# A linear-attention block times a SwiGLU block: when half of the query divisions run, the order in which a segment's right operands are split, and a priority on the first operands

## The chip, the cores and the metric

The kernel runs on one core of a Trainium2 chip. The metric is the device time of one execution in microseconds (us); lower is better. The kernel before took 2384.69 us, the median of three runs (2384.14 to 2392.65).

## The reference, cut to what matters

Shapes: x is 2048 x 1024, wqkv 1024 x 3072, wo 1024 x 1024, w1 and w3 1024 x 3584, w2 3584 x 1024, all float32; 32 heads of 32 columns.

```python
xn = layernorm(x)
q, k, v = split(xn @ wqkv)                       # per head
phi = lambda t: where(t > 0, t + 1, exp(t)) + 1e-6
kv = phi(k).T @ v;  z = sum over tokens of phi(k)
s = (phi(q) @ kv / (phi(q) @ z + 1e-6)) @ wo     # linear attention
g = silu((silu(xn @ w1) * (xn @ w3)) @ w2)       # SwiGLU
out = x + s * g
```

Both blocks, the attention that ends in s and the SwiGLU that ends in g, read the normalised x.

## The kernel before, in words

Every matrix product is float32 made of three reduced-precision matmuls (`mm3`, lines 97 to 99): each operand is split into a high part (copied by ScalarE, ACT) and a low remainder (subtracted by VectorE, DVE). On top of that, products of 2 x 2 blocks are made with seven products in place of eight: a right operand comes as B11, T2, B21, T1, T3, B22, T4, a left one as A11, S2, A12, S1, S3, S4, A22, the letters T and S being sums and differences of blocks.

**First layer** (up to line 849). Two halves of 1024 tokens, h = 0 and 1; in each, gemms for k and v, then q (4 pairs of column blocks), then gate and up, g and u (14 pairs). A gemm (`gemm`, line 399) is seven products of 12 matmuls each, in the order a, b, c, d, a, c, d: the letter is the PSUM bank, and a, c and d are accumulated into twice, so the second product on c or d waits until DVE has read the first (lines 436 and 442). Behind each product `catch_up` (line 387) advances a queue of side jobs by one step; a step is a `yield`. The jobs of half 1 are `attention_work` (line 823): denominators for the queries of half 0, the merging of kv with wo, 16 divisions for the queries of half 0 (called H0 below), denominators of half 1, and 16 divisions of half 1 (H1). `divide` (line 753) loads a tile by four DMAs on SP's queue (lines 762 and 764), waits two steps, does one DVE instruction on the loaded data (line 770) and four sums (lines 607 to 611), and stores the tile to `qs_d` from POOL's queue (line 773). Its tile has three buffers, and `go_on` loads two jobs ahead, so that a load waits until the store of the job three earlier has landed. Hidden activations go to `ho_d`; the sums of them (line 637) are stored from POOL in half 0 and from SP in half 1.

**Second layer** (from line 852): four segments B0 to B3 over the hidden columns (B0 has 2 blocks of 128 per product, the others 4), and an attention segment s. Each segment has 8 token groups m of 256 tokens, each with seven products in `ORDER` (numbered e = 0 to 6 below): 6 matmuls in B0, 12 later. The right operand of a product (`Segment.right`, line 873) lies in a buffer by its name with one copy, loaded and split in pieces of two blocks (128 x 1024), two pieces in B1 to s. The left one (`Segment.left`, line 880) comes by one DMA on SP's queue into one of five buffers, four products ahead, and is split by ACT (line 895) and DVE (line 896). While the last group (m = 7) of a segment runs, the next segment's right operands are placed, loaded and split, each right behind the product that frees its buffer (lines 1029 to 1031). DVE also reads the PSUM banks (lines 939 to 955).

The order on each engine is made when the kernel is built: a scheduler with its own simulated timeline orders the instructions by priority (program order, unless changed) and readiness. `tc.issue_after(mark)` forbids it to put the enclosed instructions ahead of the mark. At run time every engine and every DMA queue works in the order that was fixed then.

Of the kernel before, what the change touches and what calls it, by code (L numbers as in the profile page):

```python
# [9 lines left out]
F32 = mybir.dt.float32  # L10
# [6 lines left out]
P = 128  # L17
# [5 lines left out]
def tile_linear_attention_times_swiglu(  # L23
# [375 lines left out]
    def gemm(B, A, use, early=False, paired=False, own=False):  # L399
# [67 lines left out]
        next(stages, None)  # L467
        if name[0] in "gu":
            catch_up(copied, added)
# [144 lines left out]
    def hidden(h, pair):  # L614
# [18 lines left out]
        def sums(c):  # L633
            o = [small(f"hs{h}_{pair}_{c}_{e}") for e in range(2)]
            for e, _ in enumerate(four_sums(sg[0, c], sg[1, c], *o)):
                queue = nc.gpsimd if h == 0 or pair == NF // 2 - 1 else nc.sync
                queue.dma_start(out=ho_d[i][2 * h + c][:, :, 3 + 2 * e:5 + 2 * e, k],  # L637
                                in_=o[e].rearrange("p (g n s) -> p g n s", n=2, s=P))
# [113 lines left out]

    def divide(m, k):

        c, cols = m // NT, slice(m % NT * 2 * P, (m % NT + 1) * 2 * P)

        def load():
            t = job_tile([P, 4, 2 * P], f"qd{m}_{k}")
            for e in range(2):
                j = k + e * (ND // 2)  # L760
                rows = r_d[c][j * (P // DH):(j + 1) * (P // DH), cols]
                nc.sync.dma_start(out=t[:, 2 + e], in_=bass.AP(
                    tensor=rows.tensor, offset=rows.offset, ap=[[C, P // DH], [0, DH], [1, 2 * P]]))
                nc.sync.dma_start(out=t[:, e], in_=pq_d[j // JG][c][:, j % JG, cols])
            return t

        def steps(t):
            for _ in range(2):
                yield True
# [53 lines left out]
    def attention_work():  # L823
# [5 lines left out]
        work += [j for c in H1 for j in denominators(c)]  # L829
        work += [divide(m, k) for m in range(NT * H1[0], NT * NCH) for k in range(ND // 2)]  # L830
        yield from go_on(work)
# [26 lines left out]
    def late_pool(name, bufs=1):  # L858
        return ctx.enter_context(tc.tile_pool(name=name, bufs=bufs, reuse_waits="tile"))

    pacc, pu, pw, pacc2, pt, px = (late_pool(*how) for how in (
        ("pacc",), ("pu",), ("pw",), ("pacc2",), ("pt", 4), ("px", 5)))

    class Segment:
# [8 lines left out]
        def right(self, n):  # L873

            y = self.Y[n]
            for k in range(0, self.nk, 2):
                nc.sync.dma_start(out=y[:, 1, k:k + 2].bitcast(F32), in_=self.right_of(n, slice(k, k + 2)))
                split(y[:, e, k:k + 2].rearrange("p k c -> p (k c)") for e in range(2))

        def left(self, m, n):  # L880
            t = px.tile([P, 2, ND // 2, P], FR, tag="x", name=f"X{PARTNER[n]}{self.name}_{m}")
            x_ = t[:, :, :self.nk]
            loads[:] = [nc.sync.dma_start(out=x_[:, 1].bitcast(F32), in_=self.left_of(m, PARTNER[n]))]
            split(x_[:, e] for e in range(2))
            return x_
# [6 lines left out]
    def split(pair):  # L892
        hi, lo = pair
        src = lo.bitcast(F32)
        nc.scalar.copy(out=hi, in_=src)  # L895
        return nc.vector.tensor_sub(out=lo, in0=src, in1=hi.bitcast(F32))  # L896

    loads = []

# [10 lines left out]

    def temp(name):
        return pt.tile([P, C], F32, tag="t", name=name)

# [46 lines left out]
    def attention_tokens(seg, m):  # L960
# [29 lines left out]
        yield bd, True  # L990
        c22 = temp(f"c22{name}")
        A.copy(out=c22, in_=bd)
# [3 lines left out]
        yield bd, False  # L996
        c12 = temp(f"c12{name}")
        V.tensor_add(out=c12, in0=bd, in1=u)
# [16 lines left out]
    for n in PRODUCTS:  # L1015
        layers[0].place(n)
    for j, n in enumerate(ORDER):
        if j < AHEAD:
            fetch(j)
        layers[0].right(n)  # L1020
    for i, seg in enumerate(segments):
        for m in range(NG):
            parts = attention_tokens(seg, m) if seg is attention else layer_tokens(seg, m, i == 0)
            for e, n in enumerate(ORDER):
                j = (i * NG + m) * len(ORDER) + e
                fetch(j + AHEAD)
                b, start = next(parts)
                seg.product(b, X.pop(j), n, start)
                if m == NG - 1 and i + 1 < len(segments):
                    segments[i + 1].place(n)  # L1030
                    segments[i + 1].right(n)
            next(parts)
            if i == 2 and m < ADDED:
                lay_x(m)


# [21 lines left out]
```

## Time and profile before

| | |
|---|---|
| three timed runs, median | 2384.69 us |
| the profiled execution's own time | 2392.09 us |
| its span, and what lies around it | 2390.3 us, 1.8 us |
| busy: TensorE (PE), DVE, ACT, POOL | 98%, 69%, 40%, 10% of the span |
| mean granted clock of TensorE | 0.994 |
| HBM traffic over the span | 172 GB/s |

The span is the time from the first to the last instruction of one profiled execution. The profiled execution was 7.4 us longer than the median; durations are read from it, and sums are made against its own time. Windows are given in microseconds from the start of the span. PE counts as busy while matmuls that overlap run, so the number of matmuls in a window says more than the busy share. L123 is a line of the kernel before; the same statement stands one or two lines earlier or later in the kernel after. SPq is SP's DMA queue: instructions there issue transfers.

### The profile page before, as it was taken

The page shows a single profiled execution, that of the slowest core. Times are in us where ns is not written, and L with a number is a line of the kernel's source. Part 1 is how long each engine was busy: PE and PEld are TensorE (multiplying, and loading weights), DVE is VectorE, ACT ScalarE, POOL GpSimd, SP SyncE. Part 2 cuts the span into 40 slices and gives each one's busy share as a digit, 9 for nine tenths or more (in the row PEclk, how much of TensorE's full clock was granted, in tenths as well). Part 3 has the DMA queues.
Part 4 walks back from the last instruction along what each step waited for, and adds up shares of the span by engine and source line. Part 5 has one row for each costly group of instructions (what it writes and reads, how often), then busy time and mean ns, then how long its engine had stood idle before and what let it go on. Part 6 is the DMA issues. An engine that isn't in the chain of part 4 may idle for free. (4 is left out here: it accounts for less than half of the span.)

```text
span 2390.3 us, 29773 instructions
## 1 busy us (share of the span) xinstructions
PE 2338.0 (98%) x10544; PEld 1931.3 (81%) x10544; DVE 1652.1 (69%) x2941; ACT 953.5 (40%) x1612; POOL 240.6 (10%) x305
## 2 busy tenths in 40 slices
PE   6999999999999999999999999999999999999999
PEld 5788888888888888888888878887768878788787
DVE  8755878888887566567877877886564564644744
ACT  5434554433233244345343323332562342544522
POOL 3000011211212100000111110111000000000000
PEclk9999999999999999999999999999999999999999
DMA  3211455577663582134444765575463464633666
GB/s 124 88 53 54 150 172 169 187 243 243 227 232 129 189 331 106 64 105 134 166 152 168 229 211 182 166 244 180 126 215 97 140 208 150 247 97 104 229 149 157
DMA packets 289590, 395.45 MB, mean 165 GB/s; under 512 B 17008, under 2 KB 210800, under 8 KB 289328
## 3 DMA queue, kind: packets, MB, share of 16 engines
q1 hardware_dynamic: 265920, 315.67, 40.8%
q0 software_dynamic: 23520, 77.87, 9.5%
q8 instruction: 82, 1.34, 0.2%
q14 instruction: 68, 0.56, 0.1%
HBM read 271.58 MB, written 140.25 MB: 172 GB/s over the span
## 5 line engine op out<-in xcount | busy, mean ns | idle before, releaser
L629 POOL DMA_DIRECT2D ho_d<-sg x56 | 51.0, 911 | 502.2 <-DVE sg L624 439.8
L921 POOL DMA_DIRECT2D out<-acc x14 | 12.0, 861 | 683.3 <-DVE acc L969 683.3
L586 POOL DMA_DIRECT2D pq_d<-pq x32 | 17.6, 550 | 483.8 <-DVE pq L475 480.7
L637 POOL DMA_DIRECT2D ho_d<-hs x60 | 54.5, 909 | 44.8 <-DVE hs L608 30.0
L896 DVE TENSOR_TENSOR XS1B<-XS1B 128x512 fp32r<-128x512 f32 (+1 forms) x32 | 20.0, 624 | 44.5 <-ACT XS1B L895 44.5
L98 PE MATMUL aB<-B11B,XA11B 128*128 128x512 f32 x112 | 44.6, 398 | 4.2 <-DVE B11B L896 4.2
L627 POOL DMA_DIRECT2D ho_d<-sg x56 | 37.6, 672 | 101.8 <-DVE sg L624 80.6
L99 PE MATMUL dB<-T1B,XS1B 128*128 128x512 f32 x112 | 43.9, 392 | 3.9 <-DVE XS1B L896 3.9
L896 DVE TENSOR_TENSOR XA12B<-XA12B 128x512 fp32r<-128x512 f32 (+1 forms) x32 | 20.0, 624 | 37.7 <-ACT XA12B L895 37.7
L97 PE MATMUL dB<-B22B,XS4B 128*128 128x512 f32 x112 | 44.1, 394 | 1.3 <-DVE acc L939 0.7
L97 PE MATMUL aB<-B11B,XA11B 128*128 128x512 f32 x112 | 44.6, 398 | 0.6 <-ACT XA11B L895 0.6
L99 PE MATMUL cB<-T4B,XA22B 128*128 128x512 f32 x112 | 43.9, 392 | 1.3 <-DVE XA22B L896 1.3
L770 DVE SCALAR_TENSOR_TENSOR qd<-qd 128x512 f32<-128x512 f32 x32 | 21.9, 683 | 33.5 <-DMA qd<-pq_d 33.4
L99 PE MATMUL aB<-B11B,XA11B 128*128 128x512 f32 x112 | 44.5, 397 | 0.5 <-DVE XA11B L896 0.5
L97 PE MATMUL cB<-T3B,XS3B 128*128 128x512 f32 x112 | 43.8, 391 | 0.7 <-ACT cB L945 0.7
L97 PE MATMUL cB<-T4B,XA22B 128*128 128x512 f32 x112 | 43.8, 391 | 0.6 <-ACT XA22B L895 0.6
L99 PE MATMUL cB<-T3B,XS3B 128*128 128x512 f32 x112 | 43.8, 391 | 0.4 <-DVE XS3B L896 0.4
L99 PE MATMUL aB<-B21B,XA12B 128*128 128x512 f32 x112 | 43.9, 392 | 0.2 <-DVE XA12B L896 0.2
L97 PE MATMUL aB<-B21B,XA12B 128*128 128x512 f32 x112 | 43.7, 390 | 0.5 <-ACT uB L942 0.5
L99 PE MATMUL bB<-T2B,XS2B 128*128 128x512 f32 x112 | 44.1, 393 | 0.0
L97 PE MATMUL bB<-T2B,XS2B 128*128 128x512 f32 x112 | 44.0, 393 | 0.0
L98 PE MATMUL bB<-T2B,XS2B 128*128 128x512 f32 x112 | 44.0, 393 | 0.0
(5750 smaller groups left out, 8102.5 us busy)
## 6 DMA issues: line engine op xcount, KB each, us to landing
qs_d<-qd POOLq DMA_DIRECT2D x32, 512.0 KB, 5.5
ho_d<-hs POOLq DMA_DIRECT2D x60, 256.0 KB, 5.3
ho_d<-sg POOLq DMA_DIRECT2D x56, 256.0 KB, 4.2
w<-in_B_w SPq DMA_DIRECT2D x56, 256.0 KB
wt_d<-w SPq DMA_DIRECT2D x28, 512.0 KB
ho_d<-hs SPq DMA_DIRECT2D x52, 256.0 KB
pq_d<-pq POOLq DMA_DIRECT2D x32, 256.0 KB, 2.9
a_dS<-xo SPq DMA_DIRECT2D x16, 512.0 KB
```

The lines of the kernel that those rows point to most:

```text
L97: nc.tensor.matmul(acc, lhsT=wh, rhs=ah, start=start, stop=False, skip_group_check=True)
L98: nc.tensor.matmul(acc, lhsT=wh, rhs=al, start=False, stop=False, skip_group_check=True)
L99: nc.tensor.matmul(acc, lhsT=wl, rhs=ah, start=False, stop=stop, skip_group_check=True)
L586: nc.gpsimd.dma_start(out=pq_d[j // JG][2 * h + c][:, j % JG], in_=pq)
L627: nc.gpsimd.dma_start(out=ho_d[i][2 * h + c][:, :, 0, k], in_=halves[:, :, 0])
L629: nc.gpsimd.dma_start(out=ho_d[i][2 * h + c][:, :, 1:3, k], in_=halves)
L637: queue.dma_start(out=ho_d[i][2 * h + c][:, :, 3 + 2 * e:5 + 2 * e, k], in_=o[e].rearrange("p (g n s) -> p g n s", n=2, s=P))
L770: nc.vector.scalar_tensor_tensor(t[:, :2], t[:, :2], 1e-6, t[:, 2:], op0=ALU.add, op1=ALU.mult)
L896: return nc.vector.tensor_sub(out=lo, in0=src, in1=hi.bitcast(F32))
L921: nc.gpsimd.dma_start(out=out[r0:r0 + P, :].rearrange("p (n c) -> p n c", c=C), in_=a, accum_op=ALU.add)
```

## The change

Five edits:

- The 16 divisions of H1 leave `attention_work`. They become a job of their own in the second layer, with tiles from the pool `pt` (two buffers in place of three) and six steps of waiting; `catch_up` advances it by one step behind each product of the groups m = 1 to 6 in the segments B0 to B3. A division is seven steps, so 16 take 112 steps: 42 in B0, 42 in B1, 28 in B2. Each step is issued behind the newest left operand's load and split.
- The divisions of H0 stay and wait four steps in place of two.
- The gemms of q advance the side jobs by one more step (half 0 and half 1).
- The stores of the hidden sums in half 1 all go from POOL's queue (52 were on SP's).
- The right operands' pieces are still loaded at the same places, but their splits are put into a list and taken from it one or two at a time, seven in five products, from m = 7, e = 2 of the segment before to m = 0, e = 4, each behind the split of the newest left operand. The first segment's operands are issued at a higher priority.

Cut to its core:

```diff
-        if name[0] in "gu":
+        if name[0] in "guq":
             catch_up(copied, added)
...
-                queue = nc.gpsimd if h == 0 or pair == NF // 2 - 1 else nc.sync
-                queue.dma_start(out=ho_d[i][2 * h + c][:, :, 3 + 2 * e:5 + 2 * e, k],
+                nc.gpsimd.dma_start(out=ho_d[i][2 * h + c][:, :, 3 + 2 * e:5 + 2 * e, k],
...
-    def divide(m, k):
+    def divide(m, k, tile_of=job_tile, wait=4):
...
-            for _ in range(2):
+            for _ in range(wait):
                 yield True
...
-        work += [divide(m, k) for m in range(NT * H1[0], NT * NCH) for k in range(ND // 2)]
...
-                split(y[:, e, k:k + 2].rearrange("p k c -> p (k c)") for e in range(2))
+                yield lambda k=k: split(y[:, e, k:k + 2].rearrange("p k c -> p (k c)") for e in range(2))
...
-            split(x_[:, e] for e in range(2))
+            marks[:] = split(x_[:, e] for e in range(2))
...
+    def late_work():
+        yield from go_on([divide(m, k, temp, 6) for m in range(NG // 2, NG) for k in range(ND // 2)])
+
+    jobs.append((late_work(), False))
...
+    with tc.high_priority(offset=150):
+        for j, n in enumerate(ORDER):
+            if j < AHEAD:
+                fetch(j)
+            for made in layers[0].right(n):
+                made()
+
+    pending, turn = [], 0
+
+    def make_right():
+        for _ in range(7 * (turn + 1) // 5 - 7 * turn // 5):
+            if pending:
+                with ExitStack() as behind:
+                    for mark in marks:
+                        behind.enter_context(tc.issue_after(mark.ins))
+                    pending.pop(0)()
+
...
                 fetch(j + AHEAD)
+                if m == NG - 1 and e >= 2 or m == 0:
+                    make_right()
+                    turn += 1
+                else:
+                    turn = 0
                 b, start = next(parts)
                 seg.product(b, X.pop(j), n, start)
                 if m == NG - 1 and i + 1 < len(segments):
                     segments[i + 1].place(n)
-                    segments[i + 1].right(n)
+                    pending.extend(segments[i + 1].right(n))
+                elif m and i < len(layers):
+                    catch_up(*marks, *loads)
```

What it moves is seen in three places.

DVE in half 1 of the first layer, where an H0 division's first instruction (on a tile qd) meets the reads of the banks of a gemm u (c22u is read from bank c on one line and from bank d on another). Before:

```order
L436 TENSOR_TENSOR c22u1_6__11364<-cu1_6__11326,uu1_6__11306 128x512
L770 SCALAR_TENSOR_TENSOR qd2_2_11369<-qd2_2_11369 128x512
L90 TENSOR_TENSOR T3g1_7__11343<-wg1_7__11135,T3g1_7__11343 128x512
L611 TENSOR_TENSOR qd2_0_11232<-qd2_0_11232 128x128
L607 TENSOR_TENSOR qd2_2_11369<-qd2_2_11369 128x128
L610 TENSOR_TENSOR qd2_2_11369<-qd2_2_11369 128x128
L442 TENSOR_TENSOR c22u1_6__11364<-du1_6__11327,c22u1_6__11364 128x512
```

And the one place after where such an instruction follows closest on the store that its tile waits for (that of qd0_2, ten rows above this piece's fifth):

```order
L436 TENSOR_TENSOR c22u1_5__11021<-cu1_5__10989,uu1_5__10964 128x512
L90 TENSOR_TENSOR T3g1_6__11006<-wg1_6__10809,T3g1_6__11006 128x512
L442 TENSOR_TENSOR c22u1_5__11021<-du1_5__10990,c22u1_5__11021 128x512
L769 SCALAR_TENSOR_TENSOR qd0_3_10877<-qd0_3_10877 128x512
L769 SCALAR_TENSOR_TENSOR qd1_1_11095<-qd1_1_11095 128x512
L90 TENSOR_TENSOR B21g1_6__11023<-wg1_6__10809,B21g1_6__11023 128x512
L624 TENSOR_TENSOR sg1_5_11_10895<-c22u1_5__11021,sg1_5_11_10895 128x512
```

The instruction on the loaded tile stood ahead of the read of bank d; now it stands behind it.

SP's queue in B0, group 3 (an X tile is a left operand; the number behind B0 is the group). Before:

```order
L883 DMA XA12B0_3_14059<-ho_d0_1_87 128x256
L883 DMA XS1B0_3_14070<-ho_d0_1_87 128x256
L883 DMA XS3B0_3_14082<-ho_d0_1_87 128x256
L883 DMA XS4B0_3_14097<-ho_d0_1_87 128x256
L883 DMA XA22B0_3_14108<-ho_d0_1_87 128x256
```

After:

```order
L881 DMA XA12B0_3_13904<-ho_d0_1_87 128x256
L881 DMA XS1B0_3_13915<-ho_d0_1_87 128x256
L761 DMA qd4_2_13854<-r_d2_123 128x1x256
L763 DMA qd4_2_13854<-pq_d0_2_80 128x256
L761 DMA qd4_2_13854<-r_d2_123 128x1x256
L763 DMA qd4_2_13854<-pq_d1_2_84 128x256
L881 DMA XS3B0_3_13933<-ho_d0_1_87 128x256
L881 DMA XS4B0_3_13953<-ho_d0_1_87 128x256
```

The four loads of a late division now stand between two left operands; their first one waits for the store of the division two earlier. There are six such places in B0 (the first holds two divisions, the last stands between the two pieces of B11 of B1), and nine in B1 and B2.

DVE at the change from B0 to B1 (names as in the second layer, `acc` the sums, `uB` the first reader of bank b). Before:

```order
L896 TENSOR_TENSOR B11B1_14429<-B11B1_14429 128x1024 x2
L896 TENSOR_TENSOR XS4B0_7_14436<-XS4B0_7_14436 128x256
L953 TENSOR_TENSOR acc7_13788<-cB0_7_14420,acc7_13788 128x512
L896 TENSOR_TENSOR T2B1_14447<-T2B1_14447 128x1024
L955 TENSOR_TENSOR acc7_13788<-dB0_7_14421,uB0_7_14422 128x512
L896 TENSOR_TENSOR T2B1_14447<-T2B1_14447 128x1024
L896 TENSOR_TENSOR XA22B0_7_14454<-XA22B0_7_14454 128x256
L896 TENSOR_TENSOR B21B1_14466<-B21B1_14466 128x1024 x2
L896 TENSOR_TENSOR XA11B1_0_14473<-XA11B1_0_14473 128x512
L896 TENSOR_TENSOR T1B1_14484<-T1B1_14484 128x1024 x2
```

After:

```order
L893 TENSOR_TENSOR XA22B0_7_14341<-XA22B0_7_14341 128x256
L893 TENSOR_TENSOR B11B1_14324<-B11B1_14324 128x1024
L893 TENSOR_TENSOR XA11B1_0_14358<-XA11B1_0_14358 128x512
L893 TENSOR_TENSOR B11B1_14324<-B11B1_14324 128x1024
L893 TENSOR_TENSOR XS2B1_0_14374<-XS2B1_0_14374 128x512
L893 TENSOR_TENSOR T2B1_14338<-T2B1_14338 128x1024 x2
L893 TENSOR_TENSOR XA12B1_0_14392<-XA12B1_0_14392 128x512
L893 TENSOR_TENSOR B21B1_14355<-B21B1_14355 128x1024
L946 TENSOR_TENSOR uB1_0_14437<-bB1_0_14434,uB1_0_14437 128x512
L949 TENSOR_TENSOR acc0_13605<-acc0_13605,uB1_0_14437 128x512
L893 TENSOR_TENSOR XS1B1_0_14408<-XS1B1_0_14408 128x512
L893 TENSOR_TENSOR B21B1_14355<-B21B1_14355 128x1024
```

The left operands of B0 now come ahead of all right pieces of B1, and each right piece behind a left operand; five right pieces in place of eleven stand ahead of the first read of bank b (`uB1_0`).

21 lines of the change are left out of this document (8 added, 13 removed).

## The prediction

> **What bounds the kernel now.** I read the page first, then the busy times by stretches of 50 us, then TensorE's waits and the DVE and queue timelines at each wait.
>
> ```profile
> PE 2338.0 (98%) x10544; PEld 1931.3 (81%) x10544; DVE 1652.1 (69%) x2941; ACT 953.5 (40%) x1612; POOL 240.6 (10%) x305
> ```
>
> TensorE (PE) is the bound nearly everywhere, so freeing DVE is worth only what PE waits for. In the stretches that the change reaches (columns: window, its length, busy time and instructions of PE, PEld, DVE, ACT, POOL, then granted clock, DMA share, GB/s):
>
> ```profile
> 1300.00:1350.00 50.00, 50.00 (x222) 41.38 (x221) 39.34 (x82) 14.44 (x25) 9.72 (x12) 1.00 0.60 199
> 1350.00:1400.00 50.00, 46.55 (x194) 37.94 (x193) 39.72 (x87) 13.30 (x24) 9.25 (x11) 0.93 0.64 211
> 1550.00:1600.00 50.00, 48.57 (x214) 39.91 (x214) 40.84 (x89) 13.59 (x25) 10.07 (x13) 1.00 0.74 241
> 1600.00:1650.00 50.00, 47.05 (x201) 38.46 (x200) 39.96 (x86) 15.00 (x26) 8.67 (x11) 0.97 0.59 200
> 1650.00:1700.00 50.00, 45.33 (x188) 36.23 (x187) 29.90 (x51) 21.15 (x39) 7.32 (x9) 0.93 0.49 161
> 1750.00:1800.00 50.00, 44.46 (x181) 33.57 (x180) 36.40 (x48) 28.55 (x41) 0.00 (x0) 0.97 0.65 231
> 1900.00:1950.00 50.00, 48.05 (x210) 38.72 (x209) 38.49 (x51) 26.84 (x36) 0.00 (x0) 1.00 0.72 251
> 2050.00:2100.00 50.00, 47.97 (x205) 37.70 (x204) 36.17 (x48) 28.33 (x39) 0.00 (x0) 1.00 0.72 257
> 2200.00:2250.00 50.00, 48.92 (x214) 39.72 (x213) 38.50 (x50) 30.75 (x45) 0.00 (x0) 1.00 0.67 242
> ```
>
> Full pace is the first row's: 222 matmuls in 50 us, 0.225 us each. What each other row lacks to 222, times 0.225, is its loss: 6.3 us where an H0 division meets gemm u1_6, 1.8 and 4.7 at H1 divisions, 7.7 at the change of layers, 9.2 at B0 to B1, 2.7, 3.8 and 1.8 at the next three changes. Together 38.0 us: the change can hardly win more. The waits behind them (us in total, times, longest):
>
> ```profile
> PE aB L98 <- DVE B11B L896: 4.2, 1, 4.2
> PE dB L99 <- DVE XS1B L896: 3.9, 3, 1.6
> PE du__11327 L97 <- DVE c22u__11364 L442: 3.5, 1, 3.5
> PE du__13347 L97 <- DVE c22u__13384 L442: 3.0, 1, 3.0
> ```
>
> B11 is the first right operand of the second layer; the two du waits are the divisions; the XS1 waits are the segment changes.
>
> **H1's divisions leave the first layer.** On DVE (last column: idle time before, and who ended it), first the H0 case, then the H1 one:
>
> ```profile
> 1374.98 0.68 DVE L436 TENSOR_TENSOR c22u__11364<-cu__11326,uu__11306 128x512 f32<-128x512 f32 x1
> 1383.61 0.69 DVE L770 SCALAR_TENSOR_TENSOR qd<-qd 128x512 f32<-128x512 f32 x1 [7.94 <-DMA qd<-pq_d]
> ...
> 1385.42 0.68 DVE L442 TENSOR_TENSOR c22u__11364<-du__11327,c22u__11364 128x512 f32<-128x512 f32 x1
> ...
> 1628.31 0.69 DVE L770 SCALAR_TENSOR_TENSOR qd<-qd 128x512 f32<-128x512 f32 x1 [8.24 <-DMA qd<-pq_d]
> ```
>
> DVE stood 7.94 and 8.24 us on a division's load with a bank's read (L442) queued behind, and PE waited for that read. The H1 case goes altogether: of the 1.8 + 4.7 = 6.5 us all is won, or 5 if something small stays: **-6.5** (-6.5 to -5).
>
> **H0's divisions wait four steps instead of two.** The load is no earlier, it is only used later. Its tile's store and its own issue (POOL, and SP's queue):
>
> ```profile
> 1368.16 0.84 POOL L773 DMA_DIRECT2D qs_d<-qd  x1 [4.78 <-DMA qd<-pq_d]
> 1375.39 0.53 SPq L762 DMA_DIRECT2D qd<-r_d  x1
> ...
> 1377.06 0.93 SPq L764 DMA_DIRECT2D qd<-pq_d  x1
> ```
>
> From the store's issue to DVE's resumption took 1383.61 - 1368.16 = 15.4 us. In the new order the tightest case has the store's last sum some 2 us behind the read of bank d, so DVE resumes about 17.5 us behind that read; with the next split (T2 of the next gemm) 21 us behind. PE now has eight products of 12 x 0.225 = 2.7 us before it needs T2, 21.6 us, where before it had two (5.4 us) before it needed the read. So PE waits 0 to 0.5 us where it lost 6.3. I take 0.4 left: **-5.9**; to -6.5 if the wait is covered whole, and to -1 if the load is 4 us later than that and costs the clock again, as here (PEclk in the column before the last two):
>
> ```profile
> 1382.00:1386.00 4.00, 0.71 (x4) 0.24 (x2) 2.40 (x6) 0.00 (x0) 0.61 (x1) 0.89 0.03 11
> 1386.00:1392.00 6.00, 5.84 (x14) 4.59 (x15) 6.00 (x15) 0.88 (x2) 3.51 (x5) 0.50 0.52 184
> ```
>
> Behind the 3.5 us wait the clock was 0.50 for about 6 us, in which 14 matmuls ran where 6 / 0.225 = 27 would: another 2.9 us. A stall of over 3 us so costs nearly double. Shorter ones did too at the change from B0 to B1, where PE first lacked 1.26 of 2 us:
>
> ```profile
> 1758.00:1760.00 2.00, 0.74 (x3) 1.00 1.05 407
> 1760.00:1762.00 2.00, 2.00 (x6) 0.65 1.05 408
> 1762.00:1764.00 2.00, 1.52 (x4) 0.50 1.06 409
> ```
>
> The Trainium skill, "TensorE: Matmul & The Clock Gate", section "What's actually happening", has the clock halve after about one idle window of 3.4 us. The first case agrees; the second doesn't, with 0.50 reached without such a gap. By the rule alone the change from B0 to B1 would keep its clock and be some 2 us shorter (an estimate).
>
> **The loads of the late divisions stand between left operands on SP's queue.** Four loads take from 1607.94 to 1610.45 to issue, some 2.3 us beyond the first's wait; that wait, where a tile's store hadn't landed, was 91.6 / 21 = 4.4 us in the mean, and a store takes 5.5 us to land:
>
> ```profile
> 1607.94 0.56 SPq L762 DMA_DIRECT2D qd<-r_d  x1
> ...
> 1609.68 0.77 SPq L764 DMA_DIRECT2D qd<-pq_d  x1
> SPq L762 <- DMA qs_d<-qd: 91.6, 21, 10.8
> qs_d<-qd POOLq DMA_DIRECT2D x32, 512.0 KB, 5.5
> ```
>
> In B0 a product lasts 6 x 0.225 = 1.35 us, and this is the room that a left operand has (its load, its split, its first use):
>
> ```profile
> 1708.64 0.32 SPq L883 DMA_DIRECT2D XS3B<-ho_d  x1
> 1711.20 0.42 DVE L896 TENSOR_TENSOR XS3B<-XS3B 128x256 fp32r<-128x256 f32 x1 [1.03 <-ACT XS3B L895]
> ...
> 1713.88 0.39 PE L97 MATMUL cB<-T3B,XS3B 128*128 128x512 f32 x1
> ```
>
> Split done at 1711.62, used at 1713.88: 2.26 us. In the new order five left loads (6.8 us) lie between the left operand whose split the old tile's last sum follows and the new load; that sum comes some 3.5 us behind its operand's load, so the store lands at about 3.5 + 5.5 = 9 and SP waits about 2. The left load behind is late by 2 + 2.3, less the 1.35 that a step has anyway: 2.9, of which 0.7 reaches PE. Over the six places in B0, with their different distances, I take 1.0, 0.7, 0, 0.7, 0 and 1.2: **+3.5**. If no store is late: 0. If each waits the mean 4.4 us, 3.1 at each, 18.5. In B1 and B2 a product lasts 2.7 us, twice that, and I take nothing for the nine places: the step alone covers all but 2 + 2.3 - 2.7 = 1.6 us. If a store is 4 us late there too, the room of a product is still not used up. DVE, with 50 - 38.5 = 11.5 us idle in the row of 1900, takes a division (0.69 and four sums of a quarter of its columns, under 2 us) beside PE's work.
>
> **The order of the right pieces.** Nothing is removed from DVE at a change of segments; pieces are spread from products m = 7, e = 2 on, each behind a left split. Before, at B1 to B2, the left operand XS1 (waited for by PE) stood behind right pieces and readers:
>
> ```profile
> 1924.41 0.68 DVE L944 TENSOR_TENSOR uB<-bB,uB 128x512 f32<-128x512 f32 x1
> 1925.01 1.21 DVE L896 TENSOR_TENSOR B22B<-B22B 128x1024 fp32r<-128x1024 f32 x1
> ...
> 1928.48 0.68 DVE L896 TENSOR_TENSOR XS1B<-XS1B 128x512 fp32r<-128x512 f32 x1
> ```
>
> Rows follow each other by 0.60 (512 columns) and 1.13 us (1024). Now XS1 is early, and the second piece of B21 stands behind uB, acc and XS1: 3 x 0.60 + 1.13 = 2.9 us, some 3.1 with ACT's part, behind the reading of bank b, while PE has seven matmuls (1.6 us): it waits 1.5. Each piece that follows (T1, T3, B22) stands behind one more left split and one or two readers, and by the same count ends 0.35, 1.0 and 0.4 us after PE is ready for it: 3.3 in each change against 2.7, 3.8 and, at the last, 1.8 (there I take 2.6, halfway, since its readers are others). From B0 to B1 the traffic is full (408 GB/s above) and four more loads join it: 11 against 9.2. So 3.3 + 3.3 + 2.6 + 11 = 20.2 against 17.5, and with 0.6 for the pieces of B11 in products of 1.36 us: **+3.3** (-12 to +12).
>
> **The rest.** The first operands of B0 have priority, but on DVE the split of B11 still stands behind the last hidden sums: of 7.7 us nothing goes, **0** (-3 to +1). The hidden sums leave SP's queue:
>
> ```profile
> 1311.84 5.90 SPq L637 DMA_DIRECT2D ho_d<-hs  x4
> ```
>
> SP was held 5.9 us by four that waited for DVE's sums. Nothing shown waits for what came behind, so **0**; POOL is idle four fifths of the time there. That could bring H0's loads forward. The Trainium skill, "DMA: Bandwidth & Descriptors", section "Issuing engines are not separate DMA queues", speaks against it: another issuing engine saves the issue time alone. The 5.9 us are SP waiting in order, so here the row allows more; by the rule the term is nothing, which I take. The added step in q's gemms moves jobs earlier: **0** (1.5 either way).
>
> **The sum**: -6.5 - 5.9 + 3.5 + 3.3 = -5.6 us against the profiled execution, 2390.3 + 1.8 = 2392.1: 2386.5. That execution was 7.4 us above the median of 2384.69, so against the median: **2379**.
>
> **Rivals.** *The set order works* (faster): left operands are never late, and the pieces' waits are covered, since DVE has 11.5 of 50 us idle. Then the 2.7, 3.8 and 1.8 go, and a third of the 9.2, where traffic is full: 11.4 won in place of +3.3, 15 lower, **2364**. For it: PE's waits there are on XS1, which now comes first. Against: the uses of bank b and B21 follow within 1.6 us. *SP's queue stalls B0* (slower): each late division's store lands late, and SP waits the mean 4.4 us before loading at six places: 18.5 in place of 3.5, and with the clock at half behind each cluster some 10 more: 25 higher, **2404**. It decides from a store wait of about 1.3 us on, where 1.3 + 2.3 - 1.35 = 2.25 uses up the room, and costs the clock from some 4.3. For it: the mean wait of 4.4. Against: there the divisions ran closer together. *H0's wait only moves* (no change): DVE stalls as long, and PE waits at the next bank or split, 6 us kept: **2385**. For it: the load is no earlier; against it, eight products of cover.
>
> **How the numbers follow.** Forecast 0.48, the set order works 0.27, H0's wait only moves 0.15, SP stalls B0 0.10. A measurement of this kernel tells 0.5% from no change, 11.9 us: below 2372.8 or above 2396.6. Faster takes the 0.27 and 0.05 of the forecast's lower end (the order's -12): 0.32; slower the 0.10; same the rest, 0.58. The forecast's own range is 2372 (no store late, 0.4 more covered, a third of the order's -12) to 2394 (the stores' 18.5). The range over all cases goes from 2362, just below the faster rival, to 2396: it leaves out the slower rival and the far end of the faster one, about 2 in 10.
>
> **What would show it.** In the trace of the changed kernel: no wait of PE on c22u in half 1 above 1 us, and none at all past 1450 (the H1 term; one of over 3 us speaks for the moved wait). In B0, waits of PE on XS3 or XS1 with SP waiting on a store of qs_d: under 1.5 us each by the forecast, over 3 by the slower rival. At the changes of segments, PE waiting on B21, T1 or T3 instead of XS1, about 3 us in each, with 203 to 210 matmuls in their 50 us; if the count is 217 or more, the set order works. The window of the change of layers should still lose 7 to 8 us. The prediction is wrong if the two du waits are gone and the time is not below the one before, or if over 10 us were won at the segment changes.

## The result, and the profile after

The changed kernel took 2421.71 us (median of 4 runs, 2417.95 to 2424.29) against 2387.65 (4 runs, 2384.14 to 2392.65): ratio 1.014, 95% interval 1.0113 to 1.0167. It is slower, where 2379 was forecast and 2396 was the end of the range. The two profiled executions, 2417.95 and 2392.09 us, differ by 25.9; that of before was 4.4 above its median, that of after 3.8 below its own, which is the other 8 us. What follows accounts for the 25.9 (spans 2416.2 and 2390.3).

The page of the changed kernel, its busy times:

```profile
PE 2348.0 (97%) x10544; PEld 1933.3 (80%) x10544; DVE 1662.7 (69%) x2941; ACT 953.8 (39%) x1612; POOL 287.7 (12%) x357
```

PE, DVE and ACT do the same number of instructions, and POOL's 52 more are the moved stores; TensorE's share fell. By stretches of 50 us, columns as before:

```profile
1050.00:1100.00 50.00, 45.92 (x196) 37.49 (x195) 37.25 (x55) 24.51 (x43) 4.87 (x9) 0.97 0.42 138
1350.00:1400.00 50.00, 50.00 (x222) 41.41 (x221) 43.58 (x88) 15.03 (x26) 16.83 (x20) 1.00 0.56 186
1600.00:1650.00 50.00, 50.00 (x222) 41.42 (x221) 38.68 (x67) 19.25 (x35) 9.14 (x11) 1.00 0.23 86
...
1700.00:1750.00 50.00, 44.83 (x185) 34.73 (x184) 25.98 (x63) 22.21 (x54) 3.40 (x4) 0.97 0.52 166
1750.00:1800.00 50.00, 39.65 (x146) 28.55 (x146) 33.93 (x53) 28.05 (x44) 1.69 (x2) 0.90 0.71 250
1900.00:1950.00 50.00, 47.85 (x203) 38.30 (x203) 34.37 (x52) 21.49 (x32) 1.69 (x2) 0.98 0.77 269
```

The stalls at the divisions (rows of 1350 and 1600) are gone: 222 matmuls, full pace. New are a loss at 1050, where there was none, and one inside B0 (1700 to 1750; before, the trace has 221 matmuls there at full pace). The change from B0 to B1 lost more. PE's waits, the same view as before:

```profile
PE dB L97 <- ACT XS4B L893: 8.2, 2, 4.3
PE cB L97 <- ACT cB L947: 5.5, 4, 2.9
...
PE den L739 <- ACT pqs L91: 4.6, 2, 4.1
PE aB L98 <- DVE B11B L893: 4.2, 1, 4.2
PE aB L97 <- ACT B21B L893: 4.1, 3, 1.5
```

No wait on c22u is left. B11's is the old one, 4.2 us. XS4 is a left operand that came late, cB a copy on ACT, den the denominators, B21 a right operand.

Waits alone don't give the price, since the clock falls behind them. All kernels issue the same matmuls in the second layer, so their pace can be compared by number: in the timeline I take the start of the n-th matmul from the layer's first, less n times 0.2267 us (the distance of two starts at full pace). Us lost in this way, by stage; the first column is a time, from the second q gemm of half 1 to the second layer's first matmul; a change of segments runs from m = 7 to the end of m = 1 of the next, and the lower rows are the experiments below:

| kernel | second half of layer 1 | B0, m = 0 | B0, m = 1 to 6 | B0 to B1 | in B1 | B1 to B2 | in B2 | B2 to B3 | in B3 | B3 to s | s | sum of losses |
|---|---|---|---|---|---|---|---|---|---|---|---|---|
| before | 630.7 | 7.7 | 0.2 | 9.3 | 0 | 2.9 | 0 | 3.8 | 0 | 1.8 | 2.4 | 28.1 |
| changed | 625.5 | 7.3 | 15.1 | 17.3 | 2.2 | 5.3 | 1.1 | 4.6 | 0 | 5.5 | 1.5 | 59.9 |
| late from B1 | 625.3 | 7.9 | 0.6 | 11.6 | 3.5 | 6.7 | 3.6 | 7.3 | 6.6 | 5.6 | 0.3 | 53.8 |
| right at once | 626.4 | 7.4 | 14.4 | 15.5 | 4.4 | 2.5 | 1.5 | 2.0 | 0 | 2.1 | 2.8 | 52.6 |
| late loads from POOL | 625.5 | 9.9 | 9.4 | 18.6 | 0 | 11.2 | 0.9 | 6.4 | 0 | 5.7 | 1.0 | 63.1 |
| half of the late loads | 625.5 | 7.7 | 5.3 | 17.6 | 0 | 6.7 | 0 | 5.7 | 0 | 7.2 | 1.0 | 51.3 |
| three edits | 623.6 | 7.4 | 0.2 | 13.2 | 6.3 | 2.9 | 3.6 | 5.8 | 7.2 | 2.0 | 0.8 | 49.5 |
| four edits | 622.6 | 9.9 | 0.6 | 9.3 | 0.3 | 6.0 | 1.6 | 7.4 | 0 | 1.9 | 2.1 | 39.2 |
| eight late | 618.2 | 9.9 | 0.5 | 9.2 | 0 | 4.2 | 0 | 2.1 | 0 | 1.9 | 3.2 | 30.9 |
| sums from POOL only | 623.9 | 7.7 | 0.1 | 9.4 | 0 | 2.6 | 0 | 2.5 | 0 | 2.0 | 2.3 | 26.4 |
| no step in q | 622.7 | 10.2 | 15.5 | 16.8 | 2.5 | 4.6 | 1.0 | 5.1 | 0 | 5.8 | 1.5 | 63.1 |
| H0 waits two | 628.6 | 7.4 | 16.1 | 16.4 | 2.1 | 6.4 | 1.4 | 4.6 | 0 | 5.3 | 1.9 | 61.6 |
| sums on SP | 625.5 | 7.6 | 13.9 | 17.6 | 2.4 | 6.8 | 2.1 | 5.6 | 0 | 5.4 | 1.7 | 63.0 |

The edits of the last three lie in the first layer, and yet their second layer differs from the changed kernel's by up to 3 us in a cell and 3.2 in the sum, so smaller differences between rows mean little.

Changed less before: -5.2 in the first layer, +31.9 in the second, and 1.1 us earlier at the start of the first column: 25.6 of the 25.9. (The time up to half 1 varies by some 6 us from run to run with the same program there, so small differences of whole times say little, and the columns say more.)

Where B0's 15.1 come from: the first place with late divisions in the timeline, on SP's queue (first and last of eight loads, then the left operand behind them), on ACT, and on PE:

```profile
1683.37 0.57 SPq L761 DMA_DIRECT2D qd<-r_d  x1
...
1687.62 0.32 SPq L763 DMA_DIRECT2D qd<-pq_d  x1
1688.04 0.39 SPq L881 DMA_DIRECT2D XS4B<-ho_d  x1
...
1693.15 0.40 ACT L893 CAST XS4B<-XS4B 128x256 fp32r<-128x256 f32 x1 [4.15 <-DMA XS4B<-ho_d]
1693.60 0.79 PE L97 MATMUL dB<-B22B,XS4B 128*128 128x512 f32 x1 [3.88 <-ACT XS4B L893]
```

and the window behind it, in which the granted clock was 0.54 and 14 matmuls ran where 5.4 / 0.2267 = 24 would:

```profile
1693.60:1699.00 5.40, 5.40 (x14) 4.25 (x15) 2.54 (x6) 1.39 (x4) 0.00 (x0) 0.54 0.10 30
```

Two things make XS4 late. It is issued behind 4.67 us of issues, and it then takes 5.1 us (1688.04 to 1693.15) until ACT has it. Before the change, XS3's load, issued at 1708.64, reached ACT 2.1 us later:

```profile
1710.76 0.41 ACT L895 CAST XS3B<-XS3B 128x256 fp32r<-128x256 f32 x1 [1.05 <-DMA XS3B<-ho_d]
```

And hardly a store is waited for. Over B0 and the change to B1, SP's waits for stores of divided tiles are these (us in total, times, longest):

```profile
SPq L761 <- DMA qs_d<-qd: 2.3, 4, 1.5
```

At another place ACT shows a second effect:

```profile
1734.40 0.36 SPq L881 DMA_DIRECT2D XS3B<-ho_d  x1
...
1738.45 0.41 ACT L893 CAST XS3B<-XS3B 128x256 fp32r<-128x256 f32 x1 [4.56 <-DMA XS3B<-ho_d]
1738.76 0.58 ACT L947 COPY cB<-uB 128x512 f32<-128x512 f32 x1
...
1739.39 0.68 PE L97 MATMUL cB<-T3B,XS3B 128*128 128x512 f32 x1 [2.87 <-ACT cB L947]
```

ACT stands 4.56 us at the cast of a left operand that hasn't landed, and the copy that PE's next product on bank c needs stands behind it in ACT's order. The row names the copy, but the copy was only queued: its cause is XS3, which ACT had 4.05 us after its issue. At the change to B1, XS4 is late in the same way: it stands behind the four loads of the last late division in B0, and PE's 4.3 us wait on it is the longest there.

```profile
1759.18 0.41 SPq L881 DMA_DIRECT2D XS4B<-ho_d  x1
...
1765.83 0.40 ACT L893 CAST XS4B<-XS4B 128x256 fp32r<-128x256 f32 x1 [4.58 <-DMA XS4B<-ho_d]
```

### The profile page after: what moved, and what is told of

Its sections match the earlier page's. It is cut to its first block, busy times and chain, and to the rows that moved or that the text cites. A ratio compares the mean times of both kernels' runs of the same rounds, so it can differ in the third digit from the quotient of the medians.

```text
span 2416.2 us, 29757 instructions
## 1 busy us (share of the span) xinstructions
PE 2348.0 (97%) x10544; PEld 1933.3 (80%) x10544; DVE 1662.7 (69%) x2941; ACT 953.8 (39%) x1612; POOL 287.7 (12%) x357
## 4 chain that ended last, share of the span: by engine, by line
PE 88%; DMA 5%; issue 2%; DVE 2%; ACT 1%; POOL 1%; SPq 0%; DVEq 0%; ACTq 0%; POOLq 0%
PE dB L97 2%; PE dB L98 2%; PE dB L99 2%; PE cB L98 2%; PE cB L97 2%; PE aB L99 2%; PE aB L98 2%; PE cB L99 2%; PE aB L97 2%; PE kv L514 1%; PE bB L97 1%; PE bB L98 1%; PE bB L99 1%; DMA XA11s<-qs_d 1%; PE den L739 1%
## 5 line engine op out<-in xcount | busy, mean ns | idle before, releaser
L636 POOL DMA_DIRECT2D ho_d<-hs x112 | 101.8, 909 | 67.2 <-DVE hs L608 50.7
L772 POOL DMA_DIRECT2D qs_d<-qd x32 | 27.3, 857 | 437.4 <-DVE qd L611 307.3
L586 POOL DMA_DIRECT2D pq_d<-pq x32 | 17.6, 550 | 495.8 <-DVE pq L475 492.7
L97 PE MATMUL dB<-B22B,XS4B 128*128 128x512 f32 x112 | 45.0, 401 | 8.2 <-ACT XS4B L893 8.2
L98 PE MATMUL aB<-B11B,XA11B 128*128 128x512 f32 x112 | 44.3, 396 | 4.3 <-DVE B11B L893 4.2
L893 DVE TENSOR_TENSOR XA11B<-XA11B 128x512 fp32r<-128x512 f32 (+1 forms) x32 | 20.0, 624 | 40.8 <-ACT XA11B L893 40.8
L97 PE MATMUL aB<-B11B,XA11B 128*128 128x512 f32 x112 | 44.3, 396 | 3.5 <-ACT XA11B L893 3.5
L97 PE MATMUL dB<-T1B,XS1B 128*128 128x512 f32 x112 | 44.9, 401 | 1.8 <-ACT T1B L893 1.3
L97 PE MATMUL cB<-T4B,XA22B 128*128 128x512 f32 x112 | 44.5, 398 | 2.1 <-ACT XA22B L893 2.1
L98 PE MATMUL bB<-T2B,XS2B 128*128 128x512 f32 x112 | 44.4, 396 | 0.8 <-DVE T2B L893 0.8
L98 PE MATMUL dB<-T1B,XS1B 128*128 128x512 f32 x112 | 44.9, 401 | 0.1
L99 PE MATMUL dB<-B22B,XS4B 128*128 128x512 f32 x112 | 44.6, 399 | 0.0
L99 PE MATMUL dB<-T1B,XS1B 128*128 128x512 f32 x112 | 44.6, 398 | 0.0
L98 PE MATMUL dB<-B22B,XS4B 128*128 128x512 f32 x112 | 44.6, 398 | 0.0
```

The source lines that it names most:

```text
L97: nc.tensor.matmul(acc, lhsT=wh, rhs=ah, start=start, stop=False, skip_group_check=True)
L98: nc.tensor.matmul(acc, lhsT=wh, rhs=al, start=False, stop=False, skip_group_check=True)
L99: nc.tensor.matmul(acc, lhsT=wl, rhs=ah, start=False, stop=stop, skip_group_check=True)
L586: nc.gpsimd.dma_start(out=pq_d[j // JG][2 * h + c][:, j % JG], in_=pq)
L636: nc.gpsimd.dma_start(out=ho_d[i][2 * h + c][:, :, 3 + 2 * e:5 + 2 * e, k], in_=o[e].rearrange("p (g n s) -> p g n s", n=2, s=P))
L772: nc.gpsimd.dma_start(out=qs_d[m][:, :, k], in_=t.rearrange("p a (n s) -> p (a n) s", s=P))
```

## The experiments

Times are medians beside a median of the kernel before of 2389.7 to 2390.8 us on the same chips.

**Late divisions from B1 on.**

```diff
-                elif m and i < len(layers):
+                elif m and 0 < i < len(layers):
                     catch_up(*marks, *loads)
```

> The changed kernel with its late divisions begun in B1 instead of B0 (they fill B1, B2 and two thirds of B3). Theory (the loads of the late divisions, 512 KB each, hold up the left operands behind them on SP's queue, and in B0 a product of 1.36 us leaves too little room): B0 from its second group to its last loses the 14.5 us that it gained on the kernel before, the time falls from 2422 to about 2408, and B1 to B3 become at most 2 us longer. Rival (B0 is long because of the order of the right operands and the priority of the first ones, or because of DVE's work for the divisions): B0 stays within 4 us of 14.5 longer, time about 2420; or the 14.5 us come again in B1 and B2.

Measured: 2413.91 us, ratio 1.0095 (1.0076 to 1.0113). Inside B0 0.6 us are lost in place of 15.1, so it is the late divisions that B0 pays for. But B1 to B3 lose 3.5, 3.6 and 6.6, not 2 together: the left operand behind a division's loads is late there too (in B3, PE's longest wait of this kind is below), and the time fell by 8 us, not 14.

```profile
2166.20 0.50 PE L97 MATMUL aB<-B11B,XA11B 128*128 128x512 f32 x1 [3.57 <-ACT XA11B L893]
```

**No added step in q's gemms.**

```diff
-        if name[0] in "guq":
+        if name[0] in "gu":
```

> The changed kernel without the added step of the side jobs in the gemms of q. Theory (the step brings the denominators into the end of q's gemms, where PE waits 4.1 us for the scaled queries behind ACT's readers and then runs at half clock for about 2 us): the wait of the denominators' matmul goes, the first layer ends 5 to 6 us earlier, time about 2416. Rival (the denominators wait at another place, since they are only shifted): first layer within 2 us, time about 2421.

Measured: 2423.90 us (2415.03 to 2426.49), ratio 1.0129 (1.0105 to 1.0153): no gain that the time shows. The second half of layer 1 takes 622.7 us in place of 625.5. In the changed kernel the wait was this:

```profile
1086.45 0.50 PE L739 MATMUL den<-pqs,zb 128*128 128x512 f32 x1 [4.08 <-ACT pqs L91]
```

with ACT busy 4.27 of 5 us at that time (fourth of the busy columns), and the clock at 0.66 behind it:

```profile
1082.00:1087.00 5.00, 0.92 (x4) 0.49 (x3) 4.62 (x6) 4.27 (x8) 0.54 (x1) 1.00 0.18 70
1087.00:1092.00 5.00, 5.00 (x16) 3.95 (x15) 3.49 (x5) 0.65 (x2) 1.08 (x2) 0.66 0.28 106
```

Without the step it is gone there, and another comes at the second denominators:

```profile
1566.69 0.80 PE L739 MATMUL den<-pqs,zb 128*128 128x512 f32 x1 [3.78 <-ACT pqs L91]
```

```profile
1550.00:1600.00 50.00, 46.22 (x197) 37.82 (x197) 38.98 (x62) 19.43 (x33) 8.22 (x10) 0.97 0.40 139
```

So the step itself costs 2.8, and most of the wait is only shifted: between theory and rival. The stall is worth 5.9 us in the changed kernel (196 of 222 matmuls from 1050 on) and 5.6 here (197). The kernel before has neither, and no run shows which edit brings the part that stays.

**Right operands split at once.**

```diff
-                    pending.extend(segments[i + 1].right(n))
+                    for made in segments[i + 1].right(n):
+                        made()
```

> The changed kernel with the right operands split at once behind their loads, as in the kernel before, everything else as changed. Theory A (the set order of the right splits makes the changes of segment longer: each piece behind a left split comes too late for PE): the change from B0 to B1 becomes 3 to 6 us shorter and those behind it 1 to 2 us each, 6 to 10 us in all, time about 2413. Theory B (the change from B0 to B1 is longer because the late divisions' loads and stores and late left operands meet full DMA traffic there; the set order costs nothing): within 3 us of 2422, the change from B0 to B1 as long as before this edit.

Measured: 2411.16 us, ratio 1.008 (1.0062 to 1.0097), 10.5 below the changed kernel. By the table the four changes of segment are 1.8, 2.8, 2.6 and 3.4 us shorter, 10.6 in all: theory A in the sum, though least at the first change, where it put most. Inside B1, B2 and s 3.9 us come back, so the second layer gains 7.3. From B0 to B1 most of the cost stays. Two facts, late divisions in B0 or not and set order or not, make four cases; counted to the end of m = 0, ahead of the first late divisions in B1, they are 9.3 (neither: three edits, below), 11.4 (order alone: late from B1), 15.5 (late divisions in B0 alone) and 17.3 (both). The order is worth about 2, no more than such rows differ by, the late divisions 6. What of the divisions costs the 6 isn't shown: with half of their loads the change still loses 17.6, with the loads on another queue 18.6 (below). In the changed kernel, at B1 to B2, the order shows as right pieces that come too late:

```profile
1942.71 0.50 PE L98 MATMUL aB<-B21B,XA12B 128*128 128x512 f32 x1 [0.42 <-DVE B21B L893]
1945.43 0.51 PE L97 MATMUL aB<-B21B,XA12B 128*128 128x512 f32 x1 [1.29 <-ACT B21B L893]
1946.38 0.49 PE L97 MATMUL dB<-T1B,XS1B 128*128 128x512 f32 x1 [0.44 <-ACT T1B L893]
```

Behind these, at the clock's lowest (columns: PE, granted clock, DMA share, GB/s):

```profile
1948.00:1950.00 2.00, 2.00 (x6) 0.50 0.30 69
```

With the pieces at once, in the same part of the program (B1 to s), PE waits on left operands, on XA11 and, as in the kernel before, on XS1, and on no right operand:

```profile
PE aB L97 <- ACT XA11B L893: 4.4, 4, 2.0
PE dB L99 <- DVE XS1B L893: 2.1, 2, 1.1
```

**Late loads from POOL's queue** (for the late tiles alone).

```diff
-                nc.sync.dma_start(out=t[:, 2 + e], in_=bass.AP(
+                queue = nc.gpsimd if tile_of is not job_tile else nc.sync
+                queue.dma_start(out=t[:, 2 + e], in_=bass.AP(
...
-                nc.sync.dma_start(out=t[:, e], in_=pq_d[j // JG][c][:, j % JG, cols])
+                queue.dma_start(out=t[:, e], in_=pq_d[j // JG][c][:, j % JG, cols])
```

> The changed kernel with the loads of the late divisions issued from POOL's queue instead of SP's, at the same places of the program. Theory 1 (what delays the left operands is their place behind the division's loads in SP's queue, issue and transfer in order): B0 loses most of its 14.5 us, 10 or more, time about 2410. Theory 2 (the transfers themselves, 512 KB in 1 KB packets, take the DMA engines whichever queue they come from): B0 keeps over half, 8 or more of the 14.5 us, time about 2418.

Measured: 2417.49 us, ratio 1.0107 (1.0085 to 1.013). B0 keeps 9.4 of its 15.1, theory 2 by its number. The other 5.7 are not simply the price of SP's order. At the first place with its eight loads (m = 1), 6.5 us were lost and now 0; but POOL issues these eight in the first layer, 36 us earlier than SP did (first and last; so it is in the two later versions with loads from POOL):

```profile
1647.40 0.73 POOL L762 DMA_DIRECT2D qd<-r_d  x1 [10.31 <-DVE B22u__13440 L90]
...
1651.98 0.57 POOL L764 DMA_DIRECT2D qd<-pq_d  x1
```

At the places behind it (m = 2 to 6) 9.4 us are lost, against 8.7 from SP's queue: there the queue makes no difference. SP issues the left operand in its turn, and it still lands late; on SP, ACT and PE:

```profile
1729.27 0.32 SPq L882 DMA_DIRECT2D XS4B<-ho_d  x1
...
1734.79 0.40 ACT L894 CAST XS4B<-XS4B 128x256 fp32r<-128x256 f32 x1 [2.68 <-DMA XS4B<-ho_d]
1735.10 0.58 ACT L948 COPY cB<-uB 128x512 f32<-128x512 f32 x1
...
1735.74 0.50 PE L97 MATMUL cB<-T3B,XS3B 128*128 128x512 f32 x1 [2.42 <-ACT cB L948]
```

XS4 took 5.5 us, from another queue than the division's loads. PE here doesn't even need XS4 yet: it waits for the copy behind XS4's cast. In B1 and B2, where a product is twice as long, 0 and 0.9 are left. But from B1 to B2 11.2 are lost in place of 5.3, and the second layer as a whole gains nothing (63.1). The Trainium skill, "DMA: Bandwidth & Descriptors", section "Issuing engines are not separate DMA queues", says that transfers issued by different engines run on the same DMA engines and interleave. The loss at m = 2 to 6, 8.7 and 9.4 us, agrees.

**Half of the late loads.** The reciprocals' loads are left out and the DVE instruction reads the queries twice, so half of the attention result lacks its division.

```diff
+                if tile_of is job_tile:
                     nc.sync.dma_start(out=t[:, 2 + e], in_=bass.AP(
...
-            nc.vector.scalar_tensor_tensor(t[:, :2], t[:, :2], 1e-6, t[:, 2:], op0=ALU.add, op1=ALU.mult)
+            nc.vector.scalar_tensor_tensor(t[:, :2], t[:, :2], 1e-6, t[:, 2:] if tile_of is job_tile else t[:, :2],
+                                           op0=ALU.add, op1=ALU.mult)
```

> The changed kernel with the reciprocals' two loads of each late division left out, and its DVE instruction reading the queries in their place (so half of the attention's result lacks its division): two loads and 256 KB at each place in place of four and 512 KB, all instructions of the engines kept. Theory (issue and transfer of the loads delay the left operands): of the 15 us lost inside B0 under 5 stay, time about 2410. Rival (DVE's or ACT's work for the divisions, or the waits on the stores, is what B0 loses): 12 or more of the 15 stay, time about 2421.

Measured: 2410.28 us, ratio 1.0087 (1.0073 to 1.0101). Inside B0 5.3 us stay, a little over the theory's 5 and far from the rival's 12. All engines' instructions and all stores are kept, so 9.8 of B0's 15.1 are the cost of half of the loads. Whether the 5.3 left are the other half or the stores, this run doesn't tell.

**Three edits, and four.** The first three of these edits at once; then the loads from POOL's queue as well.

> Three edits at once on the changed kernel: late divisions from B1 on, no added step in q's gemms, right operands split at once. Theory (the three costs are separate and add up; the loads of the late divisions cost 1 to 2 us at each place in B1 to B3 too, because the left operand behind them lands late): second layer loses about 42 us to full pace, against 28 in the kernel before and 60 in the changed one, first layer 8 us less than before; time 4 to 8 us above the kernel before, about 2395. Rival (the edits overlap, one cost takes the place of another): time 2405 or more.

Measured: 2406.36 us, ratio 1.007 (1.0057 to 1.0082). B1, B2 and B3 lose 6.3, 3.6 and 7.2, more than the theory gave them, and the second layer 49.5, not 42. By its time the rival's case; by the columns the gains of the single edits nearly add up (59.9 - 6.1 - 7.3 = 46.5), with the late loads dearer in B1 to B3 than I took them for.

> The same three edits, and the late divisions' loads issued from POOL's queue. Theory (in B1 to B3 a product is long enough for the transfers, once the left operand's own load isn't held behind the division's four loads on SP's queue): almost nothing is lost inside B1, B2 and B3, second layer loses 28 to 32 us as in the kernel before, first layer 8 less: time 2378 to 2386, faster than the kernel before by 4 to 10 us. Rival (the transfers hold up the left operands whichever queue issues them, in B1 to B3 too): 8 us or more lost inside B1 to B3, time 2392 or more.

Measured: 2394.58 us, ratio 1.0017 (1.0004 to 1.0029). Inside the three segments 2 us are left in place of 17, as the theory says: here, unlike in B0, the queue matters. But late divisions that run until B3 meet the changes of segment, which lose 6.0 and 7.4 in place of 2.9 and 3.8, so the second layer loses 39.2 and the version is no faster than the kernel before.

**H0 waiting two steps again.**

```diff
-    def divide(m, k, tile_of=job_tile, wait=4):
+    def divide(m, k, tile_of=job_tile, wait=2):
```

> The changed kernel with the divisions of H0 waiting two steps again instead of four. Theory (the longer wait is what removed the stalls of H0's divisions, since their loads come no earlier): DVE waits on a division's load ahead of a bank's read again, PE loses 4 to 7 us in the first layer's second half, time about 2427. Rival (the stalls went because the hidden sums no longer hold SP's queue, so the loads come earlier): no stall of PE on a bank's read there, time within 2 us of 2422.

Measured: 2425.14 us, ratio 1.0155 (1.0141 to 1.0169); the second half of layer 1 takes 628.6 us, 3.0 more. DVE does wait as long as before, but PE loses little by it:

```profile
1367.62 0.70 DVE L442 TENSOR_TENSOR c22g__11220<-dg__11183,c22g__11220 128x512 f32<-128x512 f32 x1
...
1377.17 0.69 DVE L769 SCALAR_TENSOR_TENSOR qd<-qd 128x512 f32<-128x512 f32 x1 [7.04 <-DMA qd<-pq_d]
```

```profile
1312.76 0.50 PE L97 MATMUL cu__10674<-A,T4u__10602 128*128 128x512 f32 x1 [0.88 <-DVE c22u__10712 L436]
```

The 7.04 us wait stands behind the reads of its gemm's banks c and d (the second is the row at 1367.62), so its place in DVE's order keeps it from PE; of the 3.0 us about 1.2 lie at the bank read above, most of the rest at the denominators. The four steps halve DVE's waits (3.44 us is the longest in the changed kernel). What put the instruction behind the reads with two steps, this run doesn't say. The next two runs look at the stores.

**The hidden sums' stores**, back on SP in the changed kernel, and on POOL in the kernel before. The second edit is the change's own line; the first undoes it:

```diff
-                nc.gpsimd.dma_start(out=ho_d[i][2 * h + c][:, :, 3 + 2 * e:5 + 2 * e, k],
+                queue = nc.gpsimd if h == 0 or pair == NF // 2 - 1 else nc.sync
+                queue.dma_start(out=ho_d[i][2 * h + c][:, :, 3 + 2 * e:5 + 2 * e, k],
```

> The changed kernel with the stores of the hidden sums in half 1 back on SP's queue, all else as changed (H0 waits four steps, no H1 divisions in the first layer). Theory (H0's stall went because of the four steps and because H1's divisions are gone; the queue of the hidden sums is worth nothing): first layer's second half within 2 us of the changed kernel's, no wait of PE on a bank's read over 1 us, time about 2422. Rival (the sums' stores held SP's queue and made the divisions' loads late): a wait of 3 us or more comes back, 4 to 7 us lost, time about 2427.

Measured: 2421.91 us, ratio 1.0132 (1.0113 to 1.015); second half of layer 1 625.5 us, as changed. With four steps the stores' queue is worth nothing.

> The kernel before with one edit of the change alone: all stores of the hidden sums in half 1 go from POOL's queue. Theory (worth nothing by itself): both stalls at divisions stay, each within 2 us of the 6.3 and 4.7 us of before, time within 3 us of the kernel before. Rival (the sums' stores on SP made the loads late): at least one of the two stalls goes, 5 us or more faster.

Measured: 2384.74 us against 2390.81, ratio 0.9974 (0.9962 to 0.9986). Here my theory fell: the second half of layer 1 is 6.8 us shorter by this line alone. On DVE the wait of 7.94 us is 5.82, and PE's wait for the bank 0.85 in place of 3.5; the longer H1 stall stays:

```profile
1372.67 0.68 DVE L436 TENSOR_TENSOR c22u__11364<-cu__11326,uu__11306 128x512 f32<-128x512 f32 x1
1372.80 0.53 SPq L761 DMA_DIRECT2D qd<-r_d  x1
...
1379.17 0.69 DVE L769 SCALAR_TENSOR_TENSOR qd<-qd 128x512 f32<-128x512 f32 x1 [5.82 <-DMA qd<-pq_d]
```

```profile
1381.72 0.50 PE L97 MATMUL du__11327<-S,B22u__11271 128*128 128x512 f32 x1 [0.85 <-DVE c22u__11364 L442]
1620.96 0.50 PE L97 MATMUL du__13347<-S,B22u__13291 128*128 128x512 f32 x1 [3.08 <-DVE c22u__13384 L442]
```

How the line does this stays open. The stalled load is issued 0.1 us behind the start of the bank's read (L436), where it was 0.4 before, so SP's queue holds it hardly less; but DVE has it 6.4 us after that issue in place of 8.2.

The change thus has two remedies for one stall, and the stores on POOL remove most of it by themselves. The longer wait removes it without them, but that run also has the step in q and no H1 divisions, so the wait alone isn't shown.

**Only the last eight divisions late**, within B1 and with loads from POOL; three steps of waiting in the first layer, no step in q, right operands at once, sums on POOL.

```diff
-    def divide(m, k, tile_of=job_tile, wait=4):
+    def divide(m, k, tile_of=job_tile, wait=3):
...
+        work += [divide(NT * H1[0] + g, k) for g in range(NT) for k in range(ND // 2)]
...
-        yield from go_on([divide(m, k, temp, 6) for m in range(NG // 2, NG) for k in range(ND // 2)])
+        yield from go_on([divide(m, k, temp, 4) for m in range(3 * NG // 4, NG) for k in range(ND // 2)])
```

> A version built from the findings: no added step in q's gemms, right operands split at once, all divisions in the first layer wait three steps, and only the last eight run late, within B1, four steps each, with their loads from POOL's queue. Theory (each cost of the change is avoided and the stalls at divisions are removed): second layer loses 28 to 31 us to full pace as before the change, first layer's second half is 5 to 8 us shorter than before: time 2381 to 2387, 3 to 8 us faster than the kernel before. Rival (the waits come back at other places, as the denominators' did): time within 2 us of the kernel before or above it.

Measured: 2383.88 us against 2390.81, ratio 0.9974 (0.9962 to 0.9985): faster than both kernels. The second half of layer 1 is 12.5 us shorter than before, more than the 5 to 8 expected, and no wait of PE on a bank's read is left in it; these are all its waits there:

```profile
PE den L739 <- ACT pqs L91: 0.8, 1, 0.8
PE wp L97 <- ACT wos L89: 0.3, 1, 0.3
```

The second layer loses 30.9 in place of 28.1, inside B1 nothing. The one-line version with the sums from POOL has the same ratio, so which of the two is better stays open.

## Why the prediction was wrong, point by point

- **H1's divisions leave (-6.5) and H0's wait (-5.9): right in size.** Neither stall is in the trace of the changed kernel. The reason given for H0 was only part of it: with two steps the stall on PE is gone too, since DVE's instruction stands behind the bank reads, and the line that I put at 0 removes most of it by itself. Of the 12.4 us the first layer shows only 5.2, for the reason in the third point.
- **The hidden sums' stores (0): wrong by themselves, right in this company.** The step "Nothing shown waits for what came behind, so 0" failed: alone the line is worth 6.8 us; beside the four steps it is worth nothing. By the Trainium skill, "DMA: Bandwidth & Descriptors", section "Issuing engines are not separate DMA queues", another issuing engine saves the issue time alone, and the prediction took the 0 by it; the measured 6.8 us decide against that. Whether SP waiting in order, the row of 5.90 us, is what the line removes stays open.
- **The step in q's gemms (0): wrong, +2.8.** It brought the denominators' matmuls to where ACT was full. The other 4.4 of the 7.2 us missing in the first layer (12.4 - 5.2) also go with the stall at the denominators, which stays without the step. The prediction has no term for it, and its cause stays open; the version with eight late divisions doesn't have it.
- **The priority of the first operands (0): right.** The first group of B0 loses 7.3 us against 7.7, with the same 4.2 us wait on B11.
- **The loads of the late divisions (+3.5, at most 18.5): the step that failed.** It was "the left load behind is late by 2 + 2.3, less the 1.35 that a step has anyway": SP's issue and a wait on a store. The store wait was almost nothing (2.3 us in all), and the term left out was the transfer: the left operand took 4.05 to 6.65 us to ACT in place of 2.1, and 5.5 with the loads on another queue. The first place, taken at 1.0, lost 6.5: there eight loads were issued ahead of the left operand, in 4.67 us. With the clock the cost is 15.1 - 0.2 = 14.9 inside B0 and 3.3 in B1 and B2 (forecast 0). Another 6 come with the late divisions at the change to B1, 24 us in all; that these 6 are the loads' isn't shown.
- **The order of the right pieces (+3.3): right mechanism, too small.** PE waits on B21 and T1 as worked out, and the waits at B1 to B2 (0.42 + 1.29 + 0.44 = 2.2) are even below the 3.3 forecast. But the loss is 5.3 there, since the clock went to 0.50 behind them, which the prediction priced for B0 to B1 alone. By the run with the pieces split at once the order costs 10.6 at the changes, and 7.3 in the second layer as a whole.

The sum by these sizes, for the profiled pair: -5.2 in layer 1, +14.9 and +3.3 inside the segments, +8.0 from B0 to B1, +6.9 at the other three changes (2.4, 0.8, 3.7), -1.2 at the two ends of the second layer: 26.7, with 1.1 us from the start 25.6.

The slower rival named the place, B0's left operands, and the price (18.5 with clock, 25), and was given a chance of 0.10. Its mechanism, SP waiting 4.4 us for stores, is not what happened, so that its price comes near the 14.9 measured in B0 is luck. The chance was low because the only price looked at was that of a queue's instructions.

## What to carry to other kernels

Work that is moved to a place with idle engines still brings its transfers: price a load by what its bytes do to the operands behind and beside it, from issue to landing, and compare that with the room from issue to use. Where an engine works in order, ask what stands behind an operand that comes late: here a bank's copy on ACT, and PE was stopped by an operand that it didn't yet need. Count matmuls per stage rather than add up waits, since several short waits cost the clock as well.

## What was not expected of the hardware

- Waits shorter than 3 us took the clock down: behind one of 2.87 us it was 0.70 over the next 5 us (the row below, of the changed kernel), and behind three of at most 1.29 us 0.50. The Trainium skill, "TensorE: Matmul & The Clock Gate", section "What's actually happening", names an idle window of about 3.4 us. The 3.88 us wait in B0 agrees (0.54 behind it); the other two do not.

```profile
1740.00:1745.00 5.00, 5.00 (x18) 3.96 (x17) 2.84 (x7) 2.04 (x6) 0.00 (x0) 0.70 0.26 82
```

- An operand's load issued on its own queue took 5.5 us while 512 KB of division loads ran from another, against 2.1 us without them.
